# A first stage with x and W1 loaded in alternating halves on one queue

## The chip, the cores and the metric

The kernel runs on one core of a Trainium2 chip. The metric is the device time of one execution in microseconds (us), the median of several runs. The engines that matter here are TensorE (PE, with its weight loads PEld), VectorE (DVE), ScalarE (ACT), GpSimd (POOL) and SyncE (SP), whose work is almost only to issue DMAs. ACT and POOL can issue DMAs too; each engine issues its own in the order of its program.

## What is computed

x has 2048 rows (time) and 640 columns. Two branches read it, and a gate mixes them:

```python
g = sigmoid((x * gate_w).sum(-1, keepdims=True))
# branch a: a state space model, one complex state per column p
Lam_bar = exp(exp(log_dt) * Lambda)
B_bar   = ((Lam_bar - 1.0) / Lambda)[:, None] * B
h[t]    = Lam_bar * h[t - 1] + x[t] @ B_bar.T
a       = 2.0 * real(hseq @ C.T) + x * Dskip
# branch b: a dense layer, 640 -> 1728 -> 640
b       = gelu(x @ w1 + b1) @ w2 + b2
out     = g * a + (1 - g) * b
```

All inputs and the output are bf16. The change touches only how the first 512 rows of x and the first part of w1 reach TensorE.

## The kernel before, in words

The time axis is cut into four quarters q of 512 rows. For each quarter TensorE makes x @ w1 (lines 653 and 675; tails of 64 columns at 696), the input of the state space model (718), the second dense layer (1015, 809, 829) and the output of the state space model (1085, 922, 882). ACT moves results out of PSUM, with GELU after the first layer (662, 682). DVE runs the recurrence as a scan (762) with products before and after it (505).

**Order.** Every operation is declared with `op(name, engine, duration, reads, writes, fn, prio, lat)`. A planner (class `Sched`, line 33) simulates the engines with these durations and latencies, and on each engine takes, of what is ready, the smallest `prio`. That fixes the order of each engine's program. `Emitter` adds semaphore waits where another engine's result is read or a buffer is reused. Between operations of TensorE there are no waits. `load` (line 330) declares a DMA; its issue has line 333 in the profile, a transposing DMA (`load_T`) line 340.

**The first stage.** x must be transposed before it can be multiplied: `xT[q]` holds x's columns in five blocks k of 128, each with 512 time steps. For quarter 0, blocks 0 and 1 come as plain rows (`xna0`, `xna1`, 256 rows of 256 columns each, lines 369 to 371), are transposed by TensorE against an identity (428) and copied out of PSUM by DVE (434). Blocks 2 to 4 come by transposing DMAs (lines 374 and 376). W1 comes in row blocks k of 128 rows and 1024 columns (eight column blocks jf of 128), 256 KB each, `w1_1` to `w1_4` on SP's queue; `w1_0` alone is issued by ACT (line 389). The other 704 columns follow as two loads (379, 380). SP issues in this order: `xna0`, `xna1`, W1 block 1, W1 block 2, x block 2, W1 block 3, x blocks 3 and 4, W1 block 4, the rest of W1, and then the transposed B matrices.

TensorE begins with six matmuls on a constant (line 416: five of 512 columns, one of 384) whose result nobody reads; then the transposes of x's first half, a matmul of 256 columns that nobody reads (441), and the dense layer's first part (`m1_first`, line 643). That part is ordered by hand: row block 0 first, over column blocks jf 0 to 5 in half-width matmuls of 256 time steps (the first x half, then the second), (0, 6) whole, then block 1, block 2 and so on, each over its column blocks. (0, 7) and (1, 7) wait until bank 7 is free, just ahead of (2, 7). The transposes of x's second half stand, by their priority, after the third half-width matmul.

**The parameter rows.** Lambda, log_dt and b1 come as short rows into one tile `rows` (ACT's queue, lines 390 to 394); the tail of b1 is one DMA that writes the same 64 values twice. POOL zeroes the tile first (386). TensorE transposes the tile (455), DVE copies the columns (460), and exp, sin and the tables of the state space model, and the first GELU's bias, hang on that copy. Between exp, sin and GELU ACT loads an activation table each time.

Of the kernel before, what the change touches and what calls it, by code (L numbers as in the profile page):

```python
# [9 lines left out]
BF16 = mybir.dt.bfloat16  # L10
# [174 lines left out]
def bass_gated_mix__ssm_conv_s5__dense_activation_gelu__prompt_kernel(  # L185
# [18 lines left out]
    _, S, D = A_x.shape  # L204
# [21 lines left out]
    with ExitStack() as es:  # L226
# [161 lines left out]
        op("rz", "pool", 0.2, (), list(ROWS) + ["b1b", "rz"], f_rz, prio=-90)  # L388
# [12 lines left out]
        op("iota", "pool", 1.0, (), ["iota"], f_iota, prio=-60)  # L401

# [10 lines left out]
        def f_warm():  # L413
            t = None
            for n in (512,) * 5 + (384,):
# [5 lines left out]
        for i, (k, c0, c1) in enumerate(((0, 0, 2), (1, 0, 2), (0, 2, 4), (1, 2, 4))):  # L421
            bank = (7, 6, 7, 6)[i]
            pt = PS[bank][:, :].bitcast(BF16)[:, 0:(c1 - c0) * 128]

            def f_xt(k=k, pt=pt, c0=c0, c1=c1):
                t = None
                for c in range(c0, c1):
                    t = nc.tensor.transpose(pt[:, (c - c0) * 128:(c - c0 + 1) * 128], xn[0][:, c, k * 128:(k + 1) * 128], ident[:, :])  # L428
                return inc("pe", t)

            op(f"xt{i}", "pe", 0.11 * (c1 - c0), [("xna", c0 // 2), "ident"], [("bank", bank)], f_xt, prio=-990 + i if i < 2 else 3.1 + 0.1 * i)

            def f_xc(k=k, pt=pt, c0=c0, c1=c1):
                return inc("dve", nc.vector.tensor_copy(out=xT[0][:, k, c0 * 128:c1 * 128], in_=pt))

            op(f"xc{i}", "dve", 0.42, [("bank", bank)], [("xT", 0, k, c0)], f_xc, prio=-2000 + i)

        def f_fill():
            t = None
            for _ in range(1):  # L440
                t = nc.tensor.matmul(PS[3][:, 0:256], one.broadcast_to([128, 128]), one.broadcast_to([128, 256]), start=True, stop=True)
            return inc("pe", t)

        op("fill", "pe", 0.11, [("xna", 0), "ident"], [("bank", 3)], f_fill, prio=-900)
# [12 lines left out]
        op("cols", "pe", 0.3, list(ROWS) + ["b1b", "ident"], [("bank", 7)], f_cols, prio=20.5)  # L457

# [3 lines left out]
        op("cols1", "dve", 0.2, [("bank", 7)], ["lcol", "b1col"], f_cols1, prio=-1000)  # L462
# [146 lines left out]
        ctr = {"bank": 0, "pe": 0}  # L609
        held = {}  # L610

# [30 lines left out]

        def m1_first():
            late = [(0, NW - 1), (1, NW - 1)]
# [557 lines left out]
```

## Time and profile before

| what | us |
|---|---|
| median of three runs (211.71 to 212.21) | 212.1 |
| the profiled execution | 212.82 |
| its span, first to last instruction | 211.5 |
| TensorE busy (PE) | 208.8, 99% |
| DVE busy | 191.1, 90% |
| ACT busy | 102.7, 49% |
| first matmul of the warm-up starts | 0.78 |
| first transpose of x starts | 3.19 |
| first W1 matmul starts | 3.99 |
| parameter transpose (L455) starts | 8.57 |
| first GELU starts | 13.03 |
| first matmul of L675 starts | 14.24 |

Busy time is the sum over an engine's instructions. A matmul's row lists its whole way through the array, so neighbouring ones overlap, and the distance between two starts is what one costs in a stream. "Idle before" in square brackets is the time in which the engine had nothing to do, and behind the arrow stands what ended it. In the chain of waits a piece says which engine's work set the end in that stretch. In the DMA view "to landing" counts from the start of the issue to the last semaphore update of the transfer.

### The profile page before, as it was taken

To read this page: it belongs to the slowest core of one execution; us is meant where nothing else is said; L and a number is where in the kernel's file an instruction comes from. 1 tells how busy PE (TensorE), PEld (TensorE's weight loads), DVE (VectorE), ACT (ScalarE), POOL (GpSimd) and SP (SyncE) were. 2 spreads that over 40 slices of the span, in tenths; PEclk is the share of its full clock that TensorE was granted. 3 is DMA by queue.
4 is the path that set the end of the run, shared out by engine and by line. 5 is a ranking of instruction groups with operands and counts; after the bars stand their busy time and mean duration, and the time that the engine had idled before them with its cause. 6 is when DMAs were issued, how large, how long until landed. Compare 5 with 4: busy or idle time off the path is not lost.

```text
span 211.5 us, 2572 instructions
## 1 busy us (share of the span) xinstructions
PE 208.8 (99%) x1004; PEld 95.8 (45%) x1004; DVE 191.1 (90%) x244; ACT 102.7 (49%) x166; POOL 4.2 (2%) x12
## 2 busy tenths in 40 slices
PE   8999999999999999999999999999999999999996
PEld 4544444444444444444444444444444444444444
DVE  2399999999999999999999999899999999899482
ACT  2299556679860523556674222455665243304321
POOL 1000000030000000000010000000010000000000
DMA  6999899999600030043474000003742000006623
GB/s 167 275 226 147 177 186 193 384 208 186 172 0 3 0 50 0 0 84 68 99 55 110 9 3 0 0 2 67 164 83 110 0 0 3 0 2 141 137 72 99
DMA packets 50248, 19.47 MB, mean 92 GB/s; under 512 B 43068, under 2 KB 48828, under 8 KB 50236
## 3 DMA queue, kind: packets, MB, share of 16 engines
q1 hardware_dynamic: 47904, 17.59, 38.6%
q0 software_dynamic: 1600, 1.32, 4.6%
q10 hardware_dynamic: 732, 0.40, 0.7%
q8 instruction: 8, 0.13, 0.3%
q14 instruction: 4, 0.03, 0.1%
HBM read 8.68 MB, written 2.63 MB: 53 GB/s over the span
## 4 chain that ended last, share of the span: by engine, by line
PE 99%; DVE 0%; issue 0%
PE ps L675 22%; PE ps L718 20%; PE ps L1015 20%; PE ps L1085 15%; PE ps L809 5%; PE ps L653 5%; PE ps L922 4%; PE ps L829 1%; PE ps L416 1%; PE ps L696 1%; PE ps L882 1%; PE ps L1050 1%; PE ps L428 0%; PE ps L846 0%; DVE W1sb L954 0%; PE ps L844 0%
## 5 line engine op out<-in xcount | busy, mean ns | idle before, releaser
L675 PE MATMUL ps<-xT,W1sb 128*128 128x512 bf16 x220 | 48.1, 379 | 0.0
L762 DVE TENSOR_TENSOR_SCAN W<-atab,V 128x1280 bf16<-128x1280 f32 x16 | 44.3, 2812 | 0.3
L718 PE MATMUL ps<-xT,BT 128*128 128x512 bf16 x200 | 43.8, 379 | 0.0
L1015 PE MATMUL ps<-Gl,W2sb 128*128 128x512 bf16 x195 | 42.9, 379 | 0.0
L682 ACT ACTIVATE Gl<-ps,cols 128x512 bf16<-128x512 f32 x44 | 29.8, 695 | 15.5 <-PE ps L675 15.5
L675 PEld LDWEIGHTS ps<-xT,W1sb 128*128 128x128 bf16 x220 | 21.5, 98 | 26.0
L1085 PE MATMUL ps<-Hb,CT 128*128 128x512 bf16 x150 | 32.9, 379 | 0.0
L729 ACT ACTIVATE U<-ps 128x512 bf16<-128x512 f32 x40 | 23.7, 596 | 15.5 <-PE ps L718 15.5
L718 PEld LDWEIGHTS ps<-xT,BT 128*128 128x128 bf16 x200 | 19.4, 97 | 23.9 <-ACT Gt L704 0.4
L1015 PEld LDWEIGHTS ps<-Gl,W2sb 128*128 128x128 bf16 x195 | 18.9, 98 | 23.3 <-issue 0.7
L1085 PEld LDWEIGHTS ps<-Hb,CT 128*128 128x128 bf16 x150 | 14.7, 98 | 17.7
L1023 ACT ACTIVATE E1T<-ps,cols 128x512 bf16<-128x512 f32 x15 | 10.0, 686 | 26.2 <-PE ps L1015 14.7
L1093 ACT ACTIVATE E2T<-ps 128x512 bf16<-128x512 f32 x15 | 9.0, 597 | 21.7 <-PE ps L1085 21.7
L627 DVE SCALAR_TENSOR_TENSOR trf<-xn,gwb 128x640 bf16<-128x640 bf16 x16 | 13.2, 823 | 0.4
L505 DVE TENSOR_TENSOR V<-V,W 128x1280 bf16<-128x1280 bf16 x16 | 12.5, 822 | 0.3
L505 DVE TENSOR_TENSOR Hb<-Hb,V 128x1280 bf16<-128x1280 bf16 x16 | 12.5, 821 | 0.3
L505 DVE TENSOR_TENSOR V<-mr,U 128x2560 bf16<-128x2560 bf16 x8 | 11.9, 1492 | 0.3
L505 DVE TENSOR_TENSOR Hb<-c,W 128x2560 bf16<-128x2560 bf16 x8 | 11.9, 1491 | 0.2
L809 PE MATMUL ps<-W2sb,Gl 128*128 128x512 bf16 x52 | 11.9, 379 | 0.0
L505 DVE TENSOR_TENSOR V<-s,W 128x2560 bf16<-128x2560 bf16 x8 | 11.9, 1484 | 0.0
L505 DVE TENSOR_TENSOR W<-mi,U 128x2560 bf16<-128x2560 bf16 x8 | 11.9, 1484 | 0.0
L653 PE MATMUL ps<-xT,W1sb 128*128 128x512 bf16 (+1 forms) x46 | 10.2, 385 | 0.0
(103 smaller groups left out, 150.1 us busy)
## 6 DMA issues: line engine op xcount, KB each, us to landing
W2sb<-in_B_w_dram SPq DMA_DIRECT2D x1, 2080.0 KB, 8.4
out_dram<-xn SPq DMA_DIRECT2D x3, 640.0 KB, 5.0
xn<-in_A_x_dram POOLq DMA_DIRECT2D x2, 640.0 KB, 7.5
W1sb<-in_B_w_dram SPq DMA_DIRECT2D x4, 256.0 KB, 4.7
trf<-grow SPq DMA_DIRECT2D x4, 256.0 KB, 5.0
xn<-in_A_x_dram SPq DMA_DIRECT2D x1, 640.0 KB, 7.1
W1sb<-in_B_w_dram SPq DMA_DIRECT2D x1, 480.0 KB, 6.1
W1sb<-in_B_w_dram SPq DMA_DIRECT2D x1, 400.0 KB, 7.0
```

Of the source, the lines that this page charges most:

```text
L505: return inc("dve", nc.vector.tensor_tensor(out=o, in0=a, in1=b, op=o_))
L627: t = inc("dve", nc.vector.scalar_tensor_tensor(out=scr[:, :], in0=xn[q % 2][:, c, :], scalar=1.0, in1=gwb[:, :], op0=ALU.mult, op1=ALU.mu ...
L653: return inc("pe", nc.tensor.matmul(PS[jf][:, t0:t1], W1sb[:, k, jf * 128:(jf + 1) * 128], xT[0][:, k, t0:t1], start=(k == 0 and t0 == 0), ...
L675: t = nc.tensor.matmul(PS[bank][:, :], W1sb[:, k, jf * 128:(jf + 1) * 128], xT[q][:, k, :], start=(k == 0), stop=(k == KD - 1))
L682: return inc("act", nc.scalar.activation(Gl[q % 2][:, jf, :], PS[bank][:, :], ACT.Gelu_apprx_tanh, bias=b1col[:, jf:jf + 1]))
L718: t = nc.tensor.matmul(PS[bank][:, :], BT[:, ci, kd, k * 128:(k + 1) * 128], xT[q][:, kd, :], start=(kd == 0), stop=(kd == KD - 1))
L729: return inc("act", nc.scalar.activation(dst, src, ACT.Copy, scale=1.0 if ci == 0 else -1.0))
L762: t = inc("dve", nc.vector.tensor_tensor_scan(out=g[:, ci, :], data0=a, data1=v[:, ci, :], initial=0.0, op0=ALU.mult, op1=ALU.add))
L809: t = nc.tensor.matmul(PS[bank][:, :], Gl[q % 2][:, jf, t4 * 128:(t4 + 1) * 128], W2sb[:, jf, 0:DN], start=False, stop=False, skip_group_c ...
L1015: t = nc.tensor.matmul(PS[bank][:, :], W2sb[:, jf, d * 128:(d + 1) * 128], Gl[q % 2][:, jf, :], start=(jf == 0 and not lead), stop=(jf == ...
L1023: return inc("act", nc.scalar.activation(E1T[:, d, :], PS[bank][:, :], ACT.Identity, bias=cols2[:, 0, d:d + 1]))
L1085: t = nc.tensor.matmul(PS[bank][:, :].rearrange("p (s t) -> p s t", s=2), CT[:, ci, k, d * 128:(d + 1) * 128], Hb[:, 2 * (q % 2):2 * (q % ...
```

## The change

- W1's block 0 moves from ACT's queue to SP's and is cut in two: columns 0 to 511 go out behind x's first half, columns 512 to 1023 behind x's second half. SP's order becomes `xna0`, `w1_0` first half, `xna1`, `w1_0` second half, W1 block 1, and the rest as before.
- The parameter rows stay on ACT's queue, but wait for POOL's iota and for the landing of x's first half. The tail of b1 becomes two DMAs of 64 values, issued last.
- The warm-up has four matmuls of 512 columns in place of five; the fill has 384 columns in place of 256.
- Row block 0 uses half-width matmuls on column blocks 0 to 3 (eight of them) in place of 0 to 5 (twelve); blocks 4 to 6 are whole.
- TensorE's order of the whole first part is now one chain: transposes of x's first half, fill, one half-width matmul, transposes of block 0's second half, three half-width matmuls, transposes of block 1's second half, four half-width matmuls, and the whole ones as before. The parameter transpose stands in that chain just ahead of (2, 2); before it stood ahead of (2, 0).

The diff, cut to its core (the code of `x_turn`, `x_fill` and `x_cols` is that of the old loops, wrapped):

```diff
-        WSPLIT = {}
+        WSPLIT = {0: 4}
...
-                load(f"w1_{k}{i}", eng, f"l_w1{k}{i}", W1sb[:, k, f0:f1], B_w1[k * 128:(k + 1) * 128, f0:f1], [("w1", k, i)], prio=prio + 0.1 * i, lat=2.6, reads=reads)
+                load(f"w1_{k}{i}", eng, f"l_w1{k}{i}", W1sb[:, k, f0:f1], B_w1[k * 128:(k + 1) * 128, f0:f1], [("w1", k, i)], prio=prio + 0.2 * i, lat=2.0, reads=reads)
...
-                 x2[h * 256:(h + 1) * 256, 0:KN * 128].rearrange("(c p) d -> p c d", p=128), [("xna", h)], 0.2 * h, dur=0.45, lat=2.0 + 0.4 * h)
+                 x2[h * 256:(h + 1) * 256, 0:KN * 128].rearrange("(c p) d -> p c d", p=128), [("xna", h)], 0.2 * h, dur=0.45, lat=1.9)
+        w1load(0, "sp", 0.1)
         w1load(1, "sp", 1)
...
-        w1load(0, "act", -110, reads=["rz"])
-        for i, (nm, (r0, src)) in enumerate(ROWS.items()):
-            src = src.rearrange("(k p) -> k p", p=128)
-            load(nm, "act", "l_" + nm, rows[r0:r0 + src.shape[0], :], src, [nm], prio=-100 + i, dur=0.4)
-        load("b1b", "act", "l_b1b", rows[RT:RT + 1, :].rearrange("o (a p) -> o a p", a=2),
-             B_b1[nmain:F].rearrange("(o p) -> o p", o=1).unsqueeze(1).broadcast_to([1, 2, FL]), ["b1b"], prio=-101, dur=1.2)
...
+        for i, (nm, (r0, src)) in enumerate(ROWS.items()):
+            src = src.rearrange("(k p) -> k p", p=128)
+            load(nm, "act", "l_" + nm, rows[r0:r0 + src.shape[0], :], src, [nm], prio=-100 + i, dur=0.4, reads=["iota", ("xna", 0)])
+        for i in range(2):
+            load(f"b1b{i}", "act", f"l_b1b{i}", rows[RT:RT + 1, i * FL:(i + 1) * FL], B_b1[nmain:F].rearrange("(o p) -> o p", o=1), [("b1b", i)], prio=-90 + i, dur=0.4, reads=["iota", ("xna", 0)])
...
-            for n in (512,) * 5 + (384,):
+            for n in (512,) * 4 + (384,):
...
+        def first_pe(name, dur, reads, writes, fn):
+            chain.append(op(name, "pe", dur, reads, writes, fn, prio=-500 + len(chain), after=chain[-1:]))
...
-            steps = [(0, jf, h) for h in range(2) for jf in range(6)] + [(k, jf, None) for k, jf in seq if k or jf > 5]
...
+            half = lambda h: [(0, jf, h) for jf in range(WSPLIT[0])]
+            whole = [(k, jf, None) for k, jf in seq if k or jf >= WSPLIT[0]]
+            steps = [("T", 0, 0), ("T", 1, 0), ("F", 384, 0)] + half(0)[:1] + [("T", 0, 1)] + half(0)[1:] + [("T", 1, 1)] + half(1) + whole
+            steps.insert(steps.index((2, 2, None)), ("C", 0, 0))
```

More of the change, by code (lines that the diff above doesn't have):

```diff
@@ L426, in f_xt, with x_turn @@
+        def x_turn(k, h):
+            bank = 7 - k
+            pt = PS[bank][:, :].bitcast(BF16)[:, 0:256]
+            def f_xt():
                 t = None
-                for c in range(c0, c1):
-                    t = nc.tensor.transpose(pt[:, (c - c0) * 128:(c - c0 + 1) * 128], xn[0][:, c, k * 128:(k + 1) * 128], ident[:, :])
+                for c in range(2):
+                    t = nc.tensor.transpose(pt[:, c * 128:(c + 1) * 128], xn[0][:, 2 * h + c, k * 128:(k + 1) * 128], ident[:, :])
@@ L429, in f_xt @@
                 return inc("pe", t)
[L431 to L442, printed above, removed]
@@ L444, in bass_gated_mix__ssm_conv_s5__dense_activation_gelu__prompt_kernel, with f_xc, x_fill, f_fill @@
-        op("fill", "pe", 0.11, [("xna", 0), "ident"], [("bank", 3)], f_fill, prio=-900)
+            first_pe(f"xt{k}{h}", 0.22, [("xna", h), "ident"], [("bank", bank)], f_xt)
+            def f_xc():
+                return inc("dve", nc.vector.tensor_copy(out=xT[0][:, k, h * 256:(h + 1) * 256], in_=pt))
+            op(f"xc{k}{h}", "dve", 0.42, [("bank", bank)], [("xT", 0, k, 2 * h)], f_xc, prio=-2000 + 2 * h + k)
+        def x_fill(n):
+            def f_fill():
+                return inc("pe", nc.tensor.matmul(PS[3][:, 0:n], one.broadcast_to([128, 128]), one.broadcast_to([128, n]), start=True, stop=True))
+            first_pe("fill", 0.11, (), [("bank", 3)], f_fill)
@@ L464, in f_dt @@
+        m1_first()
         def f_dt():
@@ L607, in bass_gated_mix__ssm_conv_s5__dense_activation_gelu__prompt_kernel @@
         xtrans(3, range(KD), 32.7, 3.4)
-        ctr = {"bank": 0, "pe": 0}
-        held = {}
         def pe_prio():
```

57 lines of the change are left out of this document (32 added, 25 removed).

## The prediction

> **What bounds the kernel now.** I read the page's chain of waits first, by engine, and then the same chain in order of time over the first 15 us.
>
> ```profile
> PE 99%; DVE 0%; issue 0%
> ```
>
> ```profile
> 0.73 0.04 issue
> 0.78 2.61 PE ps L416 x6
> 3.39 0.43 PE ps L428 x4
> 3.82 0.21 PE ps L441
> 4.03 0.78 PE ps L653 x3
> 4.81 0.43 PE ps L428 x4
> 5.24 3.50 PE ps L653 x17
> 8.74 0.06 PE ps L455
> 8.79 5.61 PE ps L653 x26
> ```
>
> TensorE sets the end, and it works without a break from 0.78 us to the last store. So the change can save time in two ways only: TensorE does less work that nobody needs (L416 warm-up, L441 fill), or it idles less. It can lose time in one way: data that used to be early comes late. DVE matters only through what TensorE waits for: the second state block that L1085 reads at 72.91 is written by 68.92 (the timeline there: 67.36 plus 1.56), 4 us early.
>
> Next the timeline of 0 to 16 us, and one row of 4.95 to 6.74 us.
>
> ```profile
> 0.74 0.97 SPq L333 DMA_DIRECT2D xn<-in_A_x_dram  x2
> 1.75 1.09 SPq L333 DMA_DIRECT2D W1sb<-in_B_w_dram  x2
> 2.88 1.19 SPq L340 DMA_TRANSPOSE xT<-in_A_x_dram  x1
> 3.12 0.42 PEld L428 LDWEIGHTS ps<-ident,xn 128*128 128x128 bf16 x4 [0.54 <-DMA xn<-in_A_x_dram]
> 3.99 0.34 PEld L653 LDWEIGHTS ps<-xT,W1sb 128*128 128x128 bf16 x3 [0.33 <-DVE xT L434]
> ```
>
> ```profile
> 5.03 1.98 PE L653 MATMUL ps<-xT,W1sb 128*128 128x256 bf16 x9
> ```
>
> Three things are to be seen. First, the weight load of the transposes stands at 3.12 behind the landing of x's first half, but that wait is hidden: the warm-up's last matmul (2.87, 384 columns) feeds the array until 3.19, and the transposes' matmuls start at 3.19. Second, there is one real gap, 0.17 us: the fill starts at 3.61 and feeds 0.21, to 3.82; the first W1 matmul starts at 3.99, because the DVE copy of x's transposes (3.64) is not back. Third, columns are dear here. The half-width matmuls start 0.213 us apart (5.03, then 5.88 four later), 0.83 ns a column. The first whole one starts at 6.85, eight half steps and 0.11 us after 5.03, and from there 512 columns take 0.216 (5.61 us for 26), 0.42 ns a column. **So up to about 6.73 us TensorE runs at half pace** (the PEclk column reads 1.00 throughout; the steps show it). With that instant fixed, a column saved, or idle time saved, ahead of it is worth half of its own duration.
>
> Last the DMA view, narrowed to one issue at a time (KB, us from issue to landing): x's first and second half, the transposed load of x's block 2, and, from the quiet tail, a transposed load of the same 128 KB.
>
> ```profile
> xn<-in_A_x_dram SPq DMA_DIRECT2D x1, 128.0 KB, 2.3
> xn<-in_A_x_dram SPq DMA_DIRECT2D x1, 128.0 KB, 3.0
> xT<-in_A_x_dram SPq DMA_TRANSPOSE x1, 5.0
> Gl<-xT SPq DMA_TRANSPOSE x1, 2.4
> ```
>
> **Part 1, the start of the real work.** The warm-up loses one 512-column matmul: 0.43 us (its starts step by 0.427), so TensorE is free at 3.19 - 0.43 = 2.76. When has x's first half landed? Above, no later than now, 0.74 + 2.3 = 3.04 (3.12 by the weight load). Below, 2.44: the tail's small stores land 1.4 to 2.0 us after issue, and 1.7 is their middle. Now W1's 256 KB, issued at 0.97 on ACT, shares the engines with it (DMA share 0.40 at 1.5 to 2.5 us, 1.04 at 2.5 to 3.4); in the new order nothing else is issued until 1.25. I take the middle, 2.75. A matmul started 0.06 after its weight load, so the transposes start at 2.80.
>
> From there I copy the steps of before: the first W1 matmul comes 0.80 after the first transpose (3.99 - 3.19), at 3.60. The fill grows by 128 columns (0.11) and ends at 2.80 + 0.43 + 0.32 = 3.55, so 0.05 of idle remains. An SP issue costs 0.505 (two from 0.74 to 1.75), so W1's first half (128 KB) goes out at 1.25 and lands 2.0 to 2.9 later (the tail's 128 KB store; the 256 KB load of before), 3.25 to 4.15; I take 2.3, the row of the same size, 3.55. The second x half goes out at 1.75 and lands 2.0 to 3.0 later; I take 2.0, because nothing runs beside it but the queue's own order: 3.75, and it is wanted at 3.81. Then, in half pace: two transposes 0.21, three half-width matmuls 0.64, two transposes 0.21, four halves 0.85, so 3.81 + 1.92 = 5.73; W1's second half, issued at 2.26, has until then (3.5 us; 2.9 was the 256 KB row). Three whole blocks follow: 0.43 and 0.43 bring 6.59, the third crosses 6.73 and ends at 6.87. W1's second block starts at 6.87, against 6.85 + 0.22 = 7.07 before: **0.20 us earlier**. The same by accounts: 512 columns less and 128 more, 0.32; idle 0.17 less 0.05 less the 0.04 of waiting at 2.76; 0.40 at half pace, so 0.20. Eight half-width matmuls instead of twelve are the same columns; no step of the trace shows a price per instruction there, so 0.
>
> **Part 2, the later loads.** SP issues back to back, and two issues are put ahead of W1's second block: everything behind goes out 2 x 0.505 = 1.01 later. Landings now against the first weight load that needs them: W1 block 1 1.75 + 4.6 = 6.4, wanted 6.85, spare 0.5; x block 2 2.88 + 5.0 = 7.9, wanted 8.58, **spare 0.7**; x blocks 3 and 4 4.81 + 4.5 = 9.3, wanted 10.57, spare 1.3; W1 block 4 6.13 + 5.1 = 11.2, wanted 12.30, spare 1.1; W1's rest 6.75 + 6.1 = 12.9, wanted 14.03, spare 1.1. From each 0.20 goes, because TensorE is earlier, and 0.06 more at x block 2, since the parameter transpose (L455) now comes two matmuls behind it. The worst case is x block 2: spare 0.45 against a shift between 0 and 1.01, a stall of 0 to 0.55. Block 1 has 0.3 to spare, but its bytes are less delayed: W1's block 0 and x are the same 512 KB as before. The lower end is the likelier: a transposed load of this size takes 2.4 in the quiet tail and 5.0 here, so half of its 5.0 is backlog, and the DMA share is 0.8 to 1.4 from 3.4 us on. What is issued 1.01 later then waits less. I take a shift of 0.4, no stall.
>
> The Trainium skill (DMA: Bandwidth & Descriptors, Issuing engines are not separate DMA queues) says that all issuing engines share the same 16 DMA engines and that issuing from several saves only the sequencer's issue time, usually small against the transfer. By that, giving up ACT's queue costs those 1.01 us of issue and no bandwidth; by the rows, this is 1.01 against 2.3 to 5.0, not small at a spare of 0.45. Charged in full it makes the sum +0.35 instead of -0.20.
>
> **Part 3, the parameter rows.** ACT's six issues now wait for x's first half, at about 2.8. Behind them on ACT stands only the exp table load (4.07, 1.28 long), needed at 9.05. The four old issues take 1.41 (2.63 to 4.04), the split bias two more at 0.31 (a row load) to 0.59 each (half of the 1.18 it took): done by 4.8 to 5.4, the table by 6.7. The rows are wanted at 6.87 + 9 x 0.216 - 0.2 = 8.6. Their landings are not listed; the last one, issued at 3.65, was in when L455's weights loaded at 8.36, and no packet of ACT's queue is left after 7.15, so at most 3.5 us. Then 4.5 + 3.5 = 8.0: cost 0; by W1's worst 5.1 it would be 9.6, a stall of 1.0. I go by the rows' own bound.
>
> L455 moves by two matmuls, 0.43. What hangs on it is the first GELU (13.03, 0.69), which frees a bank at 13.72 for L675 at 14.24: spare 0.52, less 0.43, less what TensorE gains after L455 (nothing): 0.1 left, cost 0; without that cover at most some 0.1. DVE starts 0.2 later (0.43 less 0.20), against 4 us of slack.
>
> **Sum.** -0.20 and three zeros. Against the profiled execution (212.82, its span 211.5, so 1.3 outside) that is 212.6. Its time lies 0.7 above the median 212.1 of the three runs, and the difference carries over: **211.9**.
>
> **Rivals.**
> *A late load stalls TensorE (slower).* Place: the first matmul of W1 block 2 with x block 2. It decides from a shift of 0.45 us on, and costs what exceeds it, at full pace. With the whole 1.01 it costs 0.55, so 212.1 - 0.20 + 0.55 = 212.45; with L455's rows late by their upper end (1.0) 212.9. For it: SP issues without gaps, and the transposed issue itself takes 1.19. Against: the backlog. Chance 0.22, of which 0.06 beyond 0.64 us.
> *The half-pace stretch ends at another time.* One trace shows one instant, 6.73, 5.95 us after the first matmul. If it moves by d, the time moves by d/2. The rows bound d only widely: the end could come with the first W1 matmul (3.60, d = -3.1, 210.3), or after a second stretch as long (d = 5.95, 214.9). The nearest row is the spread of the three runs, 0.5 us, so d of about 1 either way: 211.4 or 212.4. Faster than by 0.64 it takes d = -0.9, slower by 0.64 it takes d = 1.7. For it: warm-up is cut, and idle moves. Against: that spread, and TensorE's idle time ahead of 6.73 falls from 0.17 to 0.09. Chance 0.20: 0.13 faster, 0.07 slower.
> The Trainium skill (TensorE: Matmul & The Clock Gate, Part 1) has a free-running window of about 3.4 us that must be busy before the clock doubles, so that one kernel's slow stretch varies from run to run; no trace so far shows two. By that page's figure a window missed would cost 1.7 us, as an estimate.
> *It does not do what it says:* x's first half lands at 3.04 as before. Then the transposes start at 3.10, idle grows by 0.30 behind the shorter warm-up, and 0.05 remains: 212.05. Chance 0.08.
> The forecast keeps 0.50.
>
> **How the numbers follow.** About 0.3%, 0.64 us, is what a measurement of this kernel can tell from no change. The forecast, the third rival and most of the first lie within it: 0.50 + 0.08 + 0.16 = 0.74, of which I give 0.04 to each side for the spread of 0.5 us among runs: 0.66. Faster: 0.13 + 0.04 = 0.17. Slower: 0.06 + 0.07 + 0.04 = 0.17. The range 211.2 to 212.8 takes in the forecast with that spread, the late load up to its full shift, and the earlier half of the clock's; the later clock and the late rows, and the earliest clock, are left out.
>
> **What will show it.** Right: transposes at 2.8, first W1 matmul at 3.6, W1 block 1 at 6.9, no idle of TensorE before L675. Wrong: a weight load of L653 with idle time released by a DMA of xT or W1sb; a DMA wait in front of L455; 0.213 steps that last well beyond 6.73 or end well before it; x's first half landing at 3.0. If TensorE is 0.2 earlier at L675 and the time is not, the loss is behind 20 us, where I looked for none.

## The result, and the profile after

The changed kernel takes **212.75 us** (median of 20 runs, 212.05 to 213.04), the kernel before 212.31 in the same comparison (20 runs, 211.71 to 212.79): ratio 1.0020, 95% interval 1.0013 to 1.0027. It is slower by 0.44 us; a gain of 0.20 was forecast. Both ends of the spread moved up: the fastest run by 0.34, the slowest by 0.25.

The profiled execution says the opposite at first sight: 212.05 (span 210.7) against 212.82 (211.5). The two are opposite ends of their kernels: 212.05 is the fastest run of the changed kernel, and 212.82 is longer than every one of the 20 runs of before. Whoever compares these two spans alone reads the change as a gain of 0.77.

The chain of waits of the changed kernel, by engine, and in order of time over the first 15 us (start, us, what):

```profile
PE 97%; DMA 1%; SPq 0%; DVE 0%; issue 0%
```

```profile
0.68 0.07 issue
0.74 0.46 SPq L333
1.21 0.06 issue
1.26 0.45 SPq L333
1.71 0.04 issue
1.75 2.67 DMA xn<-in_A_x_dram
4.43 0.05 issue
4.47 0.28 PE ps L435 x2
4.76 0.33 PE ps L491 x3
5.08 0.11 PE ps L435 x2
5.20 3.15 PE ps L491 x16
8.34 0.06 PE ps L460
8.40 5.21 PE ps L491 x24
...
```

Before, the chain was TensorE from 0.78 us on. Now it runs through a load: x's second half, issued at 1.75 and 2.67 us on the way, is what TensorE waited for last. From 4.47 on the chain is TensorE's alone, as before. The timeline of the same stretch shows what stood around that wait (start, length, instruction, and in brackets the idle time ahead of it and its releaser):

```profile
3.02 0.35 PEld L435 LDWEIGHTS ps<-ident,xn 128*128 128x128 bf16 x4 [0.86 <-DMA xn<-in_A_x_dram]
3.03 0.61 PE L435 MATMUL ps<-ident,xn 128*128 128x128 bf16 x4
...
3.43 0.53 PE L447 MATMUL ps<-const-bfloat16-1.0 128*128 128x384 bf16 x1
...
4.00 0.10 PEld L491 LDWEIGHTS ps<-xT,W1sb 128*128 128x128 bf16 x1 [0.52 <-DVE xT L441]
4.03 0.37 PE L491 MATMUL ps<-xT,W1sb 128*128 128x256 bf16 x1
...
4.47 0.11 PEld L435 LDWEIGHTS ps<-ident,xn 128*128 128x128 bf16 x2 [0.37 <-DMA xn<-in_A_x_dram]
...
5.14 3.20 PE L491 MATMUL ps<-xT,W1sb 128*128 128x256 bf16 x16
```

There are three gaps of TensorE in place of one. The shorter warm-up has fed the array by 2.76, the transposes start at 3.03: 0.27. The fill starts at 3.43, feeds 0.32, to 3.75, and the first W1 matmul starts at 4.03: 0.28. The bracket names DVE, but the copy that this matmul reads ended at 3.75; what came last is W1's first half, which landed at 3.90, and a weight load follows such a landing by 0.10 (4.18 and 4.28 in a trace below). That matmul has fed by 4.24, and the next transposes start at 4.47: 0.23. Together 0.78, against 0.17 before. (A fourth, 0.11 at 5.03, lies in full pace; from 5.14 on there is none.) The loads behind them, one issue each (KB, us from issue to landing), and last, from the trace of before, W1's block 1:

```profile
xn<-in_A_x_dram SPq DMA_DIRECT2D x1, 128.0 KB, 2.2
...
W1sb<-in_B_w_dram SPq DMA_DIRECT2D x1, 128.0 KB, 2.6
xn<-in_A_x_dram SPq DMA_DIRECT2D x1, 128.0 KB, 2.7
...
W1sb<-in_B_w_dram SPq DMA_DIRECT2D x1, 256.0 KB, 3.2
...
xT<-in_A_x_dram SPq DMA_TRANSPOSE x1, 3.9
```

```profile
W1sb<-in_B_w_dram SPq DMA_DIRECT2D x1, 256.0 KB, 4.6
```

x's first half lands at 2.98, W1's first half (issued 1.26) at 3.90, x's second half at 4.43. The next loads did well: W1's block 1, issued 0.99 later than before (2.74 against 1.75), lands 0.37 earlier (5.99 against 6.36), and x's block 2 took 3.9 instead of 5.0. Those behind them landed 0.1 to 0.45 later than before; the one that comes nearest to a stall is W1's block 4 (11.66 against 11.21), whose weight load waits for it; the two matmul steps around it take 0.03 more than two others.

**The half pace.** In this trace it ends at 4.5 us at the latest, in the trace of before at 6.75. That alone is worth (6.75 - 4.5) / 2 = 1.1 us, and it is why the two profiled executions differ as they do. All thirteen traces of kernels without a held start (below) obey one account. From the first matmul to the start of the first state space matmul (its line is 718 before, 733 after) TensorE works through C columns, at about 2,390 a us (256 columns step by 0.213 at half pace, 512 by 0.216 at full pace), or at half of that up to the instant u. So

start of that line = constant + C / 2390 + u / 2 + (idle before u) / 2 + (idle behind u) + (start of the first matmul) / 2.

From there on each of these kernels takes the same: profiled time less that start is 193.14 to 193.19 in every one. So the whole difference between these traces arises ahead of that line, whose start lies between 18.9 and 20.7 us. Read from the starts of single matmuls, against the trace of before (u 6.75, idle 0.09 by the same reading, which nets the gaps with steps that are shorter than their columns):

| trace | C / 2390 | u | half of idle before u | idle behind u | sum | measured |
|---|---|---|---|---|---|---|
| changed kernel | -0.16 | 4.50 | +0.31 | +0.14 | -0.84 | -0.78 |
| order alone | -0.16 | 6.32 | +0.16 | +0.06 | -0.16 | -0.16 |
| rows alone | 0 | 4.49 | 0 | +1.48 | +0.35 | +0.39 |
| loads alone | 0 | 4.30 | +0.17 | +1.07 | +0.02 | +0.08 |
| loads and rows | 0 | 4.63 | 0 | +1.10 | +0.04 | +0.09 |
| changed kernel, rows early | -0.16 | 8.46 | +0.36 | +0.06 | +1.11 | +1.10 |
| order and rows | -0.16 | 6.23 | +0.23 | +0.41 | +0.22 | +0.21 |

The sum closes to 0.07 in all. Where TensorE comes out of a gap at full pace, the trace shows only that u lies in that gap: its first transpose then steps by 0.066 for 128 columns, as behind a gap in a trace with a held start, and not by the 0.08 of half pace. So u is anywhere from 4.24 to 4.47 in the changed kernel and from 3.83 to 4.30 with the loads alone; the table goes by the upper end. The sum does not hang on it: what u / 2 loses, the two idle terms gain.

The instant u differs between traces whose TensorE did the same up to it: before, rows alone, loads alone, and loads and rows have the same matmuls at the same times (to 0.02 us) up to 3.6 us, with u at 6.75, 4.49, at most 4.30, and 4.63. It must be taken out before two kernels are compared: at an equal u the changed kernel's trace is 0.29 behind that of before (-0.16 + 0.31 + 0.14).

### The profile page after: what moved, and what is told of

The parts are those of the page before. It is cut to its first block, busy times and chain, and to the rows that moved or that the text cites. A ratio compares the mean times of both kernels' runs of the same rounds, so it can differ in the third digit from the quotient of the medians.

```text
span 210.7 us, 2570 instructions
## 1 busy us (share of the span) xinstructions
PE 207.8 (99%) x1001; PEld 94.5 (45%) x1001; DVE 191.0 (91%) x244; ACT 102.3 (49%) x166; POOL 4.2 (2%) x12
## 4 chain that ended last, share of the span: by engine, by line
PE 97%; DMA 1%; SPq 0%; DVE 0%; issue 0%
PE ps L690 23%; PE ps L733 21%; PE ps L1030 20%; PE ps L1100 15%; PE ps L824 5%; PE ps L937 4%; PE ps L491 4%; PE ps L844 1%; DMA xn<-in_A_x_dram 1%; PE ps L711 1%; PE ps L897 1%; PE ps L1065 1%; SPq L333 0%; PE ps L861 0%; PE ps L435 0%; DVE W1sb L969 0%
## 5 line engine op out<-in xcount | busy, mean ns | idle before, releaser
L1030 PEld LDWEIGHTS ps<-Gl,W2sb 128*128 128x128 bf16 x195 | 18.9, 98 | 23.3 <-issue 0.7
L1088 ACT ACTIVATE xT<-xT,cols 128x512 bf16<-128x512 bf16 x15 | 10.2, 738 | 1.8 <-DMA cols<-in_A_Dskip_dram 1.8
```

The source lines that it names most:

```text
L1030: t = nc.tensor.matmul(PS[bank][:, :], W2sb[:, jf, d * 128:(d + 1) * 128], Gl[q % 2][:, jf, :], start=(jf == 0 and not lead), stop=(jf == ...
L1088: return inc("act", nc.scalar.activation(xT[q][:, d, :], xT[q][:, d, :], ACT.Copy, scale=cols2[:, 1, d:d + 1]))
```

## Experiments

Three theories were put up. **L**: the loads at the start land later than taken, and TensorE idles. **C**: idle time and less unneeded work postpone the end of the half pace. **Q**: the two additional issues on SP make everything behind them late. All kernels compute the whole reference; the ones without a warm-up or with a longer one differ only in unneeded matmuls. Each ratio is to the kernel before, timed on the same chip in the same comparison (medians 212.25 to 212.43).

### The gaps filled

The changed kernel with its gaps filled by unneeded matmuls:

```
-            for n in (512,) * 4 + (384,):
+            for n in (512,) * 5 + (384,):
-            steps = [("T", 0, 0), ("T", 1, 0), ("F", 384, 0)] + half(0)[:1] + [("T", 0, 1)] + ...
+            steps = [("T", 0, 0), ("T", 1, 0), ("F", 480, 0)] + half(0)[:1] + [("F", 256, 0), ("T", 0, 1)] + ...
```

> The changed kernel with TensorE's idle stretches at the start covered by matmuls that nobody reads: the warm-up has its five matmuls of 512 columns again (to 3.19 us), the fill has 480 columns, and a second fill of 256 columns stands after the first W1 matmul, where the changed kernel's trace has TensorE idle until x's second half lands (4.25 to 4.47). The real work is the same and waits for the same loads. Theory L (the loads land later than I took, and only that costs): no change against the changed kernel, ratio to the kernel before 1.002. Theory C (idle TensorE time puts off, on average over runs, the instant at which the half pace ends): 0.2 to 0.3 us come back, ratio 1.0005 to 1.001. Theory Q (what SP issues 0.8 to 1.0 us later caps the runs in which the half pace ends early): ratio 1.002.

212.67 (12 runs, 212.09 to 213.04): 1.0017 (1.0007 to 1.0028). No different from the changed kernel. The trace has no idle left at the start, and its u is at 6.4, later than with the gaps. By the account no gain is due: 480 columns more than before cost 480 / 2390 = 0.20 us, and the idle that they replace, less the columns that the changed kernel saves, cost 0.15 at half value (worked out below). **C gets no support: the time that it forecast to come back did not.** It is not refuted either, because the interval reaches down to 1.0007, into its range of 1.0005 to 1.001.

### No warm-up at all

The kernel before without the L416 matmuls:

```
-        op("warm", "pe", 2.7, (), [("bank", 4)], f_warm, prio=-1000)
```

> The kernel before without its warm-up (the six matmuls of line 416, whose result nobody reads, are left out); all else is as before, and x's first half still lands at about 3.1 us. Theory L: the instant at which the half pace ends does not hang on what TensorE did, so nothing changes: ratio 1.000. Theory C: the instant needs a stretch of work behind it, and 2.4 us of work are gone: it comes up to 2.4 us later, up to 1.2 us lost, ratio 1.003 to 1.006, and the trace's 0.213 us steps last beyond 7 us.

213.59 (7 runs, 212.51 to 213.77): 1.0047 (1.0029 to 1.0066). In the trace the first matmul is at 3.01 and u at 7.31, against 6.75 with the warm-up. That trace is of a run of 213.04, below the median. In the account the 2,944 columns that are left out (-1.23) and the later first matmul (+1.12) nearly cancel, so the 1.3 us between the medians stand for an instant some 2.6 us later, as an estimate. So the end of the half pace does depend on earlier work: C holds in the gross case, where all 2.4 us of warm-up are gone.

### W1's block 0 back on ACT's queue, in halves

```
-        w1load(0, "sp", 0.1)
...
+        w1load(0, "act", -110, reads=["rz"])
```

> The changed kernel with W1's block 0 (still in two halves) issued by ACT, at 0.97 us and 0.45 later, as before the change; SP issues x's two halves back to back and everything behind them 1.0 us earlier than in the changed kernel. Theory L: x's second half lands at about 4.3 instead of 4.43, W1's first half by 3.6 instead of 3.90: some 0.1 us back, ratio 1.0015. Theory C: TensorE's idle time falls from 0.8 to about 0.5: 0.1 to 0.2 back, ratio 1.001 to 1.0015. Theory Q: the whole loss of 0.44 us comes back, ratio 1.000.

212.81 (5 runs, 212.69 to 213.23): 1.0033 (1.0020 to 1.0045). All of SP's later loads go out 1 us earlier, and it is no faster than the changed kernel: **as the whole of the loss, Q falls.** None of the three forecasts was met. (In the changed kernel's own trace, too, TensorE has no gap behind 5.14.) A part is not excluded by this run, because a new gap stands in it:

```profile
3.90 0.39 PE L491 MATMUL ps<-xT,W1sb 128*128 128x256 bf16 x1
5.11 0.29 PE L435 MATMUL ps<-ident,xn 128*128 128x128 bf16 x2 [0.81 <-DMA xn<-in_A_x_dram]
```

x's second half, issued at 1.27 between the two W1 halves of the other queue (0.97 and 1.40), landed at 5.06, 3.8 us later; TensorE stood for 1.0 us (the bracket counts from the listed end of the row before, which lies behind the end of its feed). W1's second half, issued 0.13 behind it, landed 0.18 ahead of it: which of two queues' loads arrives first is not set here by the order of issue.

### The old warm-up and fill kept

The changed kernel with five 512-column warm-up matmuls and the 256-column fill of before:

```
-            for n in (512,) * 4 + (384,):
+            for n in (512,) * 5 + (384,):
-            steps = [("T", 0, 0), ("T", 1, 0), ("F", 384, 0)] + ...
+            steps = [("T", 0, 0), ("T", 1, 0), ("F", 256, 0)] + ...
```

> The changed kernel with the warm-up and the fill of the kernel before (five matmuls of 512 columns, fill of 256): one part of the change undone alone. x's first half landed at 2.98 and W1's first half at 3.90 in the changed kernel, so the longer warm-up (to 3.19) delays no real matmul. Theory L and theory Q: no change against the changed kernel, ratio 1.002. Theory C: 0.27 us of idle time at 2.76 to 3.03 is covered, ratio 1.001 to 1.0015.

212.20 (12 runs, 211.90 to 213.11): 1.0007 (0.9993 to 1.0021). Seven runs are at 212.22 or below, five at 212.57 or above. It is between the two kernels, and the interval holds both 1.000 and the changed kernel's 1.0020: inconclusive.

### Two attempts at a start with the clock already up

To take the half pace out of the comparison, all loads were held behind a chain of DVE copies while 35 to 37 warm-up matmuls ran, in the kernel before and the changed one alike, once with two small additional loads on SP (for Q), once with rows that do not wait:

```
...
+        gate = op("gate", "dve", 9.5, (), [("H", 0), ("H", 1), ("H", 2), ("H", 3)], f_gate, prio=-9000)
...
-            return op(name, eng, dur, reads, writes, fn, prio=prio, lat=lat, after=after)
+            return op(name, eng, dur, reads, writes, fn, prio=prio, lat=lat, after=list(after) + [gate])
...
-            for n in (512,) * 5 + (384,):
+            for n in (512,) * 37:
...
+            load(f"two{i}", "sp", f"l_two{i}", two[:, i, :], x2[0:128, 16 * i:16 * i + 16], [("two", i)], 0.5 + 0.1 * i)
```

> The kernel before, held back: DVE first does a zeroing and five copies of 1280 elements on scratch (some 9 us, no part of the result), and every load waits for the last of them; TensorE's warm-up is lengthened to 37 matmuls of 512 columns, so that it works through the whole wait and the half pace is over when x lands. From there the program is that of before. All theories: with the clock out of play the spread of runs, 1.0 us in both kernels, should shrink to 0.4 or less if it comes from the instant at which the half pace ends. It is the base for the next three; only differences among the four count.

> The changed kernel, held back in the same way (35 warm-up matmuls: two fewer, the same 0.43 us less at full pace). Theory L: the loads of the first slabs land 0.1 to 0.5 us later relative to the first issue than before, TensorE at full pace must wait for W1's block 1 in both kernels anyway, so 0 to 0.2 us above o1. Theory Q: the transposed loads and W1's block 4, issued 0.8 us later, set TensorE's pace at full clock: 0.4 to 0.8 us above o1. If it is below o1, the order of loads is no loss by itself and the loss of 0.44 us lies in how it meets the clock.

> o1 with two tiny loads (128 x 32 bytes each, into a tile that nobody reads) on SP's queue behind x's halves, so that SP issues all that follows about 1.0 us later, with hardly any bytes more. Theory Q: 0.4 to 0.9 us above o1, as o2. Theory L: 0 to 0.2 above o1.

> o2 with the parameter rows not waiting for x's first half: that part of the change undone alone. Theories L and Q: the same as o2 within 0.1 us. If the rows are late at full pace, up to 0.5 us below o2, and the parameter transpose no longer waits in the trace.

With five copies the hold was too short (the loads went out at 6.5, and the warm-up set the pace until 11). Before 218.74, changed 218.90, two issues 219.57, rows free 218.47, each from 4 or 5 runs with a spread of 0.5 to 1.2 us: the instant u, 4.4 to 6.4 in these traces, still decides. This set failed for its purpose. By its median the run with two issues is 0.83 above its base, as Q forecast; but the two traces differ by 0.09 in time and by 0.2 in u, half of which is 0.1, so nothing is left for Q in them. One thing came of the set: the changed kernel and its twin with free rows have the same work and no late load, and their traces differ by 0.97 in u and by 0.47 in time. That is the half again.

> o1 again with nine copies in place of five: o1's hold was too short (it ended at 6.5 us, and the warm-up, which lasts to 10.9, set the pace), so that no load was late there. Now the loads go out at about 10.0, x's first half lands at about 12.3, and TensorE is through its warm-up by 11.7 at the latest. Full pace from the first transpose on. Base for the next two. The spread of runs should now be that of the loads alone, 0.5 us or less.

> o2 again with nine copies. Theory L: 0 to 0.3 us above p1 (the second half of x and W1's block 1 land at about the same time after the first issue in both). Theory Q: 0.4 to 0.8 above p1, with weight loads that wait for the transposed x blocks or W1's block 4.

> o3 again with nine copies: p1 with two tiny loads on SP's queue ahead of W1's block 1. Theory Q: 0.4 to 1.0 us above p1. Theory L: 0 to 0.2.

With nine copies: before 222.57 (two runs at 221.85, two at 223.4 and 223.3 with a granted clock of 0.992), changed 221.02, two issues 222.50 (two runs at 221.8 and 221.9, two at 223.2 and 223.4 with the clock of 0.992), all of 4 runs. Two additional SP issues in front of W1's block 1 cost nothing (1.0493, 1.0462 to 1.0524, against 1.0483, 1.0452 to 1.0514): Q is not borne out a second time. The changed loads are 0.8 us better here, at a granted clock of 1.000, where L had forecast them 0 to 0.3 above the loads of before and Q 0.4 to 0.8 above. In the traces x's first half takes 2.2 us with them and 3.5 with the loads of before. There ACT issues W1's 256 KB only 0.07 us behind x, where the ordinary start gives 0.23 (0.97 against 0.74) and x's first half takes 2.3. So the changed loads protect x from W1 in a case that the ordinary start does not have; that the short distance is the reason was not tried by itself.

### The parts of the change, one by one and in pairs

The change has three parts: the **loads** (W1's block 0 in halves on SP), the **order** (TensorE's steps with warm-up and fill), and the **rows** that wait. Each run below takes those it names into the kernel before, or, for the pair of loads and order, gives the changed kernel the rows of before.

```
 loads:  -        WSPLIT = {}
         +        WSPLIT = {0: 4}
         ...
         +        w1load(0, "sp", 0.1)
         ...
         -        w1load(0, "act", -110, reads=["rz"])
 rows:   +            load(nm, "act", "l_" + nm, ..., reads=["iota", ("xna", 0)])
         +        for i in range(2):
         +            load(f"b1b{i}", "act", f"l_b1b{i}", ..., reads=["iota", ("xna", 0)])
 order:  -            for n in (512,) * 5 + (384,):
         +            for n in (512,) * 4 + (384,):
         ...
         +            steps = [("T", 0, 0), ("T", 1, 0), ("F", 384, 0)] + half(0)[:1] + [("T", 0, 1)] + ...
```

> The kernel before with the loads of the change alone: W1's block 0 in two halves on SP's queue between and behind x's halves, ACT's queue free of it; warm-up, fill, half-width matmuls on six column blocks and the parameter rows as before. The planner now puts four half-width matmuls ahead of the transposes of x's second half, not three and not one. The loads land as in the changed kernel, but TensorE's work covers the time until they do: warm-up to 3.19, four half-width matmuls until 4.84. Theory L (idle TensorE time at the start is the loss): ratio 1.000. Theory Q (later loads): 1.001 to 1.002, as in the changed kernel.

> The kernel before with only TensorE's part of the change: one warm-up matmul less, the longer fill behind the transposes, x's second-half transposes between the half-width matmuls, eight of these instead of twelve, the parameter transpose two matmuls later. Loads and parameter rows as before. If the changed kernel loses because its loads land late (theory L), this kernel has before's loads: W1's block 0 in time, x's second half at about 3.7, and the order should cost only what the shorter warm-up leaves bare behind the first transposes: 0.1 to 0.3 us of idle at half value, ratio 1.000 to 1.001. If the order itself loses (theory C: less unneeded work at the start moves the end of the half pace), ratio 1.002 or more and a later instant of half pace.

> The kernel before with only the rows' part of the change: the parameter rows wait for the iota and for x's first half, and the split bias goes as two loads. x's second half, W1's block 0 and block 1 then have the transfers to themselves. In the kernel before these are all in time already (block 1 lands at 6.36 and is wanted at 6.85), so theory L says 1.000 (0.999 to 1.0005), with W1's block 1 landing up to 1 us earlier. If the later rows cost something (a wait in front of L455, or the first GELU late), 1.001 or more and TensorE shows idle at or behind L455.

> The kernel before with the change's loads and its waiting rows, but TensorE's order and warm-up as before. Loads alone gave 1.0051 with W1's block 1 landing at 7.09, 0.8 us late. If it was the rows beside them that made block 1 late, then here block 1 lands at about 6.0 to 6.3, no idle stands before it, and the ratio is 1.000 to 1.002: what is left is x's second half and W1's first half, each about 0.2 to 0.4 late at half value. If the rows have nothing to do with it, 1.004 to 1.006 again, with block 1 at about 7.1.

> The changed kernel with the parameter rows as before, started at once on ACT and not waiting. If the rows' transfers delay W1's block 1 (theory L with the rows as the cause), it lands at about 7 instead of 6.0 and TensorE stands idle before it for 0.6 to 0.9 us: ratio 1.004 to 1.005. If the wait of the rows does nothing, 1.002 as the changed kernel.

> TensorE's order (with its shorter warm-up) and the waiting rows of the change, but the loads as before: the last of the eight combinations. Rows alone gave 1.0041 with TensorE idle for 0.79 us in front of the parameter transpose (L455), whose rows were late; order alone 1.0015. If the rows' wait is harmful wherever W1's block 0 stays whole on ACT's queue, the parameter transpose waits again, for 0.4 to 0.8 us at full pace: ratio 1.003 to 1.005. If the two matmuls by which the order moves that transpose back cover it, 1.000 to 1.002.

| parts | median us (runs) | ratio | 95% interval | where TensorE waits in the trace |
|---|---|---|---|---|
| order | 212.61 (12) | 1.0015 | 0.9995 to 1.0036 | 0.30 behind the shorter warm-up |
| rows | 213.19 (5) | 1.0041 | 1.0029 to 1.0053 | 0.79 before L455, 0.30 before W1 block 1 |
| loads | 212.95 (12) | 1.0051 | 1.0026 to 1.0076 | 0.86 before W1 block 1, 0.47 before the first W1 matmul |
| loads and rows | 212.72 (11) | 1.0024 | 1.0015 to 1.0033 | 0.67 before W1 block 1 |
| loads and order | 213.04 (6) | 1.0045 | 1.0027 to 1.0062 | 0.66 before the first W1 matmul |
| order and rows | 213.03 (12) | 1.0038 | 1.0021 to 1.0054 | 0.58 before the transposes, 0.35 before the parameter transpose |
| all three | 212.75 (20) | 1.0020 | 1.0013 to 1.0027 | 0.78 in three gaps, above |

No part is measurably faster alone, and no pair is. Single runs of three of these kernels lie 1 to 2 us higher: three of twelve with the loads alone (214.57 to 215.09), one of twelve with the order alone (214.79), two of twelve with order and rows (214.11 and 214.31); no trace shows one. The ratios go by all runs; by the medians the loads alone are at 1.0033.

*Loads alone* (nothing else held back; L had forecast 1.000): W1's first half takes 2.9 us instead of 2.6, with the row loads beside it, and block 1, issued at 2.97, lands at 7.09. The waits of the weight loads in its trace (total, times, longest):

```profile
PEld ps L653 <- DMA W1sb<-in_B_w_dram: 1.1, 1, 1.1
```

*Rows alone*: theory L expected no change, and TensorE waits for the rows (0.79 from the end of the feed before it). It also waits 0.30 for W1's block 1, which lands at 6.35 as in the trace of before (6.36): with u at 4.49 the loads of before are not all in time either.

```profile
9.35 0.22 PE L455 MATMUL ps<-ident,rows 128*128 128x128 bf16 x1 [0.63 <-DMA rows<-in_B_b_dram]
```

The last row is issued at 5.28 and the last packet of ACT's queue ends at 8.74, 3.5 us later; with order and rows at 8.57. With the change's loads the same rows are issued at 5.18 and are through at 6.94 (changed kernel), 7.46 (loads and rows). What differs ahead of the rows is when SP issues x's transposed block 2: at 2.74 to 2.75 where the rows are late (8.74, 8.57, and 7.86 with both W1 halves on ACT), at 3.21 to 3.69 where they are through by 6.7 to 7.5. The two go together in all eight traces without a held start that have waiting rows. But in the three late ones ACT's queue also carries all of W1's block 0, and in the others half of it or none; which of the two is the cause was not tried.

*Loads and order, rows early*: the rows push W1's first half to 4.18 (3.90 in the changed kernel), TensorE stands for 0.66 ahead of 4.31, and here the half pace lasts to 8.46. The weight loads behind show it, 0.43 apart for 512 columns up to 8.20:

```profile
4.28 0.10 PEld L492 LDWEIGHTS ps<-xT,W1sb 128*128 128x128 bf16 x1 [0.90 <-DVE xT L442]
...
6.92 0.15 PEld L492 LDWEIGHTS ps<-xT,W1sb 128*128 128x128 bf16 x1 [0.28 <-issue]
7.35 0.15 PEld L492 LDWEIGHTS ps<-xT,W1sb 128*128 128x128 bf16 x1 [0.28 <-issue]
7.78 0.15 PEld L492 LDWEIGHTS ps<-xT,W1sb 128*128 128x128 bf16 x1 [0.28 <-issue]
8.20 0.15 PEld L492 LDWEIGHTS ps<-xT,W1sb 128*128 128x128 bf16 x1 [0.28 <-issue]
8.55 0.96 PEld L492 LDWEIGHTS ps<-xT,W1sb 128*128 128x128 bf16 x5 [0.19 <-issue]
```

Whether idle time moved the instant here stays open. There are 0.9 us of it between 2.76 and 4.60, against at least 0.55 ahead of the instant in the changed kernel's trace, which came by 4.47. But the run with both W1 halves on ACT idles for 1.4 us between 2.76 and 5.10 and is at full pace from there; where in its last gap (4.11 to 5.10) the half pace ended, its trace cannot show. One trace each cannot tell a threshold.

What the pairs say: **the rows' wait seems to pay only together with the loads** (1.0051 to 1.0024 without the new order, 1.0045 to 1.0020 with it). The intervals of the first pair overlap and those of the second touch, so the times alone do not show it; the traces give the reason, since with the wait ACT's queue is empty while W1's first half comes (2.6 against 2.9 us). Without the loads the wait costs 0.4%, and 0.2% with the new order, where the intervals overlap. The rows' wait repairs some of what the loads break, and what is left is 0.2%.

### W1's first half on ACT, the old warm-up

The changed kernel with the warm-up and fill of before, and W1's first half as ACT's first load, so that x's second half goes out at 1.27:

```
-        w1load(0, "sp", 0.1)
+        w1load(0, "sp", 0.1, only=1)
...
+        w1load(0, "act", -110, reads=["rz"], only=0)
```

> The changed kernel with the old warm-up and the old fill (as in the run that kept the warm-up, 1.0007), and W1's block 0 first half as ACT's first load (0.97) instead of SP's second: x's second half goes out at 1.26 instead of 1.75, W1's second half third on SP, everything behind 0.5 earlier. Theory L: W1's first half lands at 3.4 to 3.7 and x's second half at 3.9 to 4.3, so that at most 0.3 us of idle is left at the start: ratio 0.998 to 1.000. If the engines serve two queues at once no faster than one, x's second half lands at 4.4 to 5.1 as in the run with both halves on ACT, and the ratio is 1.001 to 1.003.

212.58 (12 runs, 212.27 to 213.03): 1.0009 (0.9998 to 1.0021), where L had 0.998 to 1.000. Here every load is in time: W1's first half at 3.37, x's second half at 3.72, W1's block 1 at 6.02, ACT's last packet at 7.06.

```profile
3.61 0.42 PE L450 MATMUL ps<-const-bfloat16-1.0 128*128 128x256 bf16 x1
3.99 0.39 PE L494 MATMUL ps<-xT,W1sb 128*128 128x256 bf16 x1
4.18 0.42 PE L438 MATMUL ps<-ident,xn 128*128 128x128 bf16 x2
4.39 0.85 PE L494 MATMUL ps<-xT,W1sb 128*128 128x256 bf16 x3
5.03 0.42 PE L438 MATMUL ps<-ident,xn 128*128 128x128 bf16 x2
5.24 3.83 PE L494 MATMUL ps<-xT,W1sb 128*128 128x256 bf16 x16
```

The first W1 matmul starts at 3.99, as before, and the only gap is the 0.16 of before. **With the data in time and the unneeded columns as before, the trace is that of before**: apart from u, the account leaves 0.05 us between them. That is what L asks of the trace. The time cannot confirm it: the interval holds 1.000, and at its edge the changed kernel's 1.0020, and the run with the old warm-up and the late loads measured the same (1.0007). So no run shows by its time alone that the late landings are the loss. In a trace with a late instant the kernel before had no more to win from its loads than half of 0.17 us. No version tried here is measurably faster than the kernel before.

## Why the prediction was wrong, step by step

**Part 1, the landings: the step that failed.** The sum needed three landings. x's first half was taken at 2.75 (the middle of 2.44 and 3.04) and came at 2.98. W1's first half was taken at 2.3 us ("the row of the same size") and took 2.64. x's second half was taken at 2.0, "because nothing runs beside it but the queue's own order", and took 2.67. The first is the middle of its range, the second lies in the lower half of its own, the third at the lower end, and the choices add up. In place of 0.09 of idle (0.04 + 0.05) there are 0.78. Put into the account: columns saved 0.32, idle lost 0.78 - 0.17 = 0.61, at half value (0.61 - 0.32) / 2 = **+0.15 instead of -0.20**. That is the sign of the result, and 0.35 of the 0.64 us between forecast and measurement, worked out from the one trace at the prediction's own instant. The other numbers of the same step held: the copies bring the first W1 matmul 0.8 behind the transposes if its weights are there (the trace: 1.00, of which 0.2 is the wait for W1), and eight half-width matmuls cost what twelve do per column.

Better rows were there: in the trace of before itself, 128 KB behind another 128 KB and W1's block took 3.0. Over the six traces with this order of loads on SP (the changed kernel, gaps filled, warm-up kept, loads alone, loads and rows, loads and order) x's second half takes 2.5 to 2.8 and W1's first half 2.6 to 2.9; the row of 2.0 came from stores in a quiet tail.

**The instant of the half pace** was held fixed at 6.73. The arithmetic (a column or idle time ahead of it is worth half) held in every trace; the assumption of one instant did not. Across the traces it is at most 4.3 to 6.75, with 7.31 where TensorE began late and 8.46 with the rows early. The working took the sum from a profiled execution 0.7 above the median, and carried that difference over as a constant. By the account it is the late instant of that execution. With an early one TensorE catches up with its loads, and then late data cost their full time, not half (0.67 us before W1's block 1 in the trace of loads and rows). What remains of the 0.44 beyond the 0.15, 0.29 us (0.13 to 0.42 by the interval), fits with that, since both ends of the spread of runs moved by about as much; but a run without a profile shows neither its instant nor its landings, and it **stays open** how much each has of it.

**Part 2, the later loads: right in its trace, and partly by luck.** Taken were a shift of 0.4 and no stall. W1's block 1 and x's block 2 landed earlier than before (5.99 against 6.36, 7.54 against 7.86), though issued 0.99 and 0.81 later; the loads behind them landed later by up to 0.45, as taken. The spare is thin: the weight load of x's block 2 waits 0.17 us for it, hidden behind the matmul that still runs, and W1's block 4, for which the text had a spare of 1.1, came just in time. And it is not safe: with the same issues, block 1 landed at 6.89 in the run with loads and rows. The Trainium skill (DMA: Bandwidth & Descriptors, Issuing engines are not separate DMA queues) makes the issue time the only loss from giving up ACT's queue; the held start with two more SP issues (1.0493 against 1.0483) and the run with both halves on ACT agree that this loss is not what counts here. That the placing of W1 moves only issue time is not what the traces show: x's second half issued at 1.27 lands at 3.72 with 128 KB of W1 on ACT, at 4.14 to 4.43 with 256 KB in one load, at 5.06 with two loads of 128 KB.

**Part 3, the rows: right for the whole change, for a reason that I had not seen.** The cost is 0: the last row packet ends at 6.94 (4.5 + 3.5 = 8.0 was the bound), and the parameter transpose starts at 8.18 without a wait. I priced only the wait's harm. Its use is to keep W1's first half free of the rows (0.3 us), and its harm, 0.79 us before L455, appears where the loads are those of before. The two matmuls by which L455 moves and the GELU chain cost nothing: there is no gap of TensorE from 5.14 us on.

**The rivals.** *A late load stalls TensorE* had its place at x's block 2; the late loads were those at the very start. *It does not do what it says* named the condition that came true (x's first half at 3.0), with 0.08 and a price of 0.15, and stopped there: the same lateness in the two loads behind it was not thought of. *The half-pace stretch ends at another time* described the spread of the runs (1.1 us among 20, so 2.2 us of instant, if that is all of it) but not the difference of the two kernels. The Trainium skill (TensorE: Matmul & The Clock Gate, Part 1) has the window of about 3.4 us that runs freely of the program; by it the end of the half pace comes one to two windows after TensorE became busy, as an estimate 4.2 to 7.6 us here. Eleven of the twelve traces with a warm-up and without a held start fit that (6.75 at the latest); the twelfth, with the rows early, has 8.46.

## What to carry to other kernels

Where a start is at the clock's half pace, a matmul cut from the warm-up gains nothing if the data that end the warm-up do not come sooner: first read from the trace what the first loads take among each other, and take the slowest comparable row, not the middle. Before two profiled executions are compared, take out what moves by itself between runs (here the instant of the clock, half of it in time); a profile can show a kernel as faster by 0.8 us which is slower by 0.4. Try the parts of a change one by one and in pairs: here no part alone is faster, and the whole loses less than the loads or the rows by themselves.

## What the runs showed of the hardware

- The end of the half pace is not set by the matmuls alone: with the same matmuls at the same times up to 3.6 us it came at 6.75, 4.63, 4.49 and at most 4.30, and by the account half of such a difference is in the time. The times of one kernel spread over 1.0 to 1.1 us; without a warm-up the runs fall into two groups, 212.5 to 213.0 and 213.6 to 213.8.
- Idle of at least 0.55 us between 2.76 and 4.47 went with full pace from 4.47 on, 1.4 us between 2.76 and 5.10 with full pace from 5.10 on, and 0.9 us between 2.76 and 4.60 with half pace until 8.46 (one trace each).
- Five short row loads on another queue (0.2 to 3.2 KB each) beside a 128 KB load go with 0.3 us more for it (2.9 against 2.6), and rows that wait for x's first half are through 1.5 to 3.5 us behind their last issue.
- The same issues land differently in different executions: W1's block 1, issued at 2.74 in four traces, landed at 5.99, 6.04, 6.23 and 6.89.
